# Softmax sums and tap weights in two PSUM tiles, fewer GpSimd taps, wider weight conversions, and an earlier start for four token-mixing tiles

## The chip, the cores and the metric

The kernel runs on one core of one Trainium2 chip. The metric is device time in microseconds (us) of one execution, median of three runs. Engines are named as in the profile: PE (TensorE matmul) and PEld (its weight load), DVE (VectorE), ACT (ScalarE), POOL (GpSimd), SP (SyncE, which here only issues DMAs). A trailing q, as in ACTq, is the engine's queue of DMA issues.

## The reference

Three blocks run one after the other on x of 4 batches, 4224 tokens and 192 features, in fp32.

```
# 1. convolution with weights per token: 8 heads, 7 taps
w = softmax(weight_gen, axis=-1)                    # (4, 4224, 8, 7)
x[b,s,h,:] = sum_k w[b,s,h,k] * x_pad[b, s+k, h, :]
# 2. Fourier mixing and an MLP
mixed = real(fft(fft(x, axis=1), axis=2))
u = x + mixed
x = u + relu(layernorm(u) @ w_ch1) @ w_ch2          # 192 -> 768 -> 192
# 3. token mixing by two 4224 x 4224 matrices
theta = x @ w_theta
y = w_tok_r @ (x*cos(theta)) + w_tok_i @ (x*sin(theta))
u = x + y
out = u + relu(u @ w_ch)
```

The large matrices arrive as fp64 words (passed as int64) and are converted on the chip.

## The kernel before

**Prologue.** Block 1 goes in 32 steps, `g` = 0 to 31: 4 batches of 8 chunks, each chunk 4 or 5 tokens on each of the 128 partitions. Two chunks share one tile `w` of tap weights (`load_w(d)`, d = g // 2). Its softmax is six instructions on DVE and one on ACT: the maximum over the 7 taps (L111), subtract (L113), the exponential on ACT (L114), the sum (L116), add 1e-9 (L118), reciprocal (L120), multiply (L122). The maxima and sums are in `m`, 64 or 72 columns in SBUF. `pool_taps(g)` lets POOL multiply and add the first `NPOOL[c]` of the 7 taps (3 or 4) into `pa` and lets ACT copy the chunk's weights to PSUM (`wps`, L151). `dve_taps(g)` does the rest on DVE: per tap two half-width multiplies (L169), whose weights come from `wps`, and two adds (L178), with two more adds (L174) that take in POOL's `pa`. After the instructions of `dve_taps` whose count is in `SOFT`, one piece of the next softmax is emitted, and after every second one a `step` of the Fourier transforms: `rotated` and `spectrum` on PE, copies on ACT, and joins into `mxt` on DVE (L252, L256). Each engine takes its instructions strictly in the order in which the code emits them.

**Start of the main phase.** `main_phase` walks over steps t, from `T0` = -86. At each t every active generator emits one piece. For t below 0 these are the transforms of the last batch, the conversion of the small weights from fp64 words to a pair of floats, high and low part (`weight`, through `convert`: five ACT and four DVE instructions for each tile, 6 tiles of 256 and 9 of 192 columns), and `prep(k)` for the first token blocks: layer norm, MLP, theta, sine and cosine, and the operand `z`. Block k holds token group k // 2 and batch pair k % 2; `BEGIN` sets its first step, and `load_x(k)` fetches its data. Blocks 0 and 2 hold batches 0 and 1. Blocks 1 and 3 hold batches 2 and 3 and need the last transform, block 3 through DRAM (`mxd`). Tiles `x` have two buffers there.

**Main stream.** From t = 0 PE multiplies `z` by converted tiles of the token matrices (`ws`, 704 columns; `conv(n)` converts tile n, `load_w(n)` fetches its words into `raw`, two buffers) into `y` (L844), one slot of two steps after the other, and DVE adds `y` into `acc` (L431, L433). Slots 0 to 11 use batch pair 0 and the tiles 0 to 3, slots 12 to 23 pair 1 and the same tiles. In this kernel `conv(0)` to `conv(3)` begin at t = -12, -6, 0 and 6 (`2 * u[2] - CONV_STEPS[u[3]]`). This stream runs to the end of the kernel, with `prep` of the later blocks beside it.

Of the kernel before, what the change touches and what calls it, by code (L numbers as in the profile page):

```python
# [10 lines left out]
F32 = mybir.dt.float32  # L11
# [8 lines left out]
PSUM = bass.MemoryType.PSUM  # L20
DRAM = bass.MemoryType.DRAM

B, S, D, H, K, DFF = 4, 4224, 192, 8, 7, 768
P = 128
# [2 lines left out]

SEQ = ((0, 5), (29, 4), (5, 4), (25, 4), (9, 4), (21, 4), (13, 4), (17, 4))
XO = [sum(n + 6 for _, n in SEQ[:c]) for c in range(9)]
SOFT = (0, 1, 4, 6, 8, 10)  # L30
NPOOL = (3, 3, 4, 3, 3, 4, 3, 4)
TCH = 352
NCH = S // TCH
HCH = NCH // 2
PAIR_STEPS = 36
LEAD = 20
BEGIN = {0: -72, 2: -54, 1: -36, 3: -8}
T0, TM, TF = -86, -40, -35
SPARE = (2, 3)
HEAD = 4  # L40
FFT_STEPS = 1
MLP_STEPS = ((13, 14, 17), (15, 16, 19), (18, 19, 22), (21, 22, 25), (24, 25, 28), (27, 28, 31))
NRAW = 2
CONV_STEPS = (18, 12)
BLOCKS = ((0, 0), (1, 0), (0, 1), (1, 1), (2, 1), (1, 2), (2, 2))
OFF = [(31 * j) % 128 if j < NF else (127 - 31 * j) % 128 for j in range(NJ)]
INV2PI = 0.15915494309189535
# [13 lines left out]
def prologue(tc, I, xs, mx, state):  # L61


    nc = tc.nc
    fctx, wctx, actx = ExitStack(), ExitStack(), ExitStack()
# [8 lines left out]
    xp = pool(actx, "px", 3)  # L74
    wp = pool(actx, "pw", 2)
    gp = pool(actx, "pg", 2)
    ps_w = pool(actx, "psw", 2, space=PSUM)
    ps_t = pool(actx, "pst", 3, space=PSUM)

    const = cp.tile([P, NCONST], F32, name="const")  # L80
# [2 lines left out]
    DI = const[:, 844:1100]  # L83
    BD = [const[:119, 1100 + 119 * i : 1219 + 119 * i] for i in range(3)]

    xin, wn, xn, taps = {}, {}, {}, {}
    queue = state["queue"] = collections.deque()

    def load_x(g):
# [7 lines left out]
    def load_w(d):  # L97
        b, c = divmod(d, 4)
        g0, n = 8 * (8 * c + (c > 0)), 8 * (8 + (c == 0))
        w = wp.tile([P, 9 * H, K], F32, tag="w", name=f"w{d}")  # L100
        nc.scalar.dma_start(
            out=w[:, :n].rearrange("p g k -> p (g k)"), in_=I["wg"][b, :, g0 * K : (g0 + n) * K]
        )
        wn[d] = (w, n)

    def softmax(d):
        w, n = wn[d]
        w = w[:, :n]
        m = wp.tile([P, 9 * H], F32, tag="m", name=f"m{d}")[:, :n]
        wide = m.unsqueeze(2).to_broadcast([P, n, K])  # L110
        nc.vector.tensor_reduce(out=m, in_=w, axis=AX.X, op=ALU.max)  # L111
        yield
        nc.vector.tensor_tensor(out=w, in0=w, in1=wide, op=ALU.subtract)  # L113
        nc.scalar.activation(w, w, AF.Exp)  # L114
        yield
        nc.vector.tensor_reduce(out=m, in_=w, axis=AX.X, op=ALU.add)  # L116
        yield
        nc.vector.tensor_scalar(m, m, 1e-9, None, op0=ALU.add)  # L118
        yield
        nc.vector.reciprocal(m, m)  # L120
# [18 lines left out]
    def pool_taps(g):  # L139
        b, c, n, d, jl = place(g)  # L140
        nt = NPOOL[c]
        pa = gp.tile([P, 5, D], F32, tag="pa", name=f"pa{g}")
        for k in range(nt):
            t = pa if k == 0 else gp.tile([P, 5, D], F32, tag="pb", name=f"pb{g}{k}")
            nc.gpsimd.tensor_tensor(  # L145
                out=hv(t, 0, n, None), in0=hv(xin[g], k, n, None), in1=wv(wn[d][0], jl, n, k), op=ALU.mult
            )
            if k:
                nc.gpsimd.tensor_tensor(out=pa[:, :n], in0=pa[:, :n], in1=t[:, :n], op=ALU.add)  # L149
        wps = ps_w.tile([P, 5 * H, K], F32, tag="wps", name=f"wps{g}")  # L150
        nc.scalar.copy(wps[:, : n * H], wn[d][0][:, jl * H : (jl + n) * H])  # L151
        taps[g] = (nt, pa, wps)

    def dve_taps(g):
        b, c, n, d, jl = place(g)
        nt, pa, wps = taps.pop(g)
        if c % 2 == 0:
            xn[d] = np_.tile([P, 9, D], F32, tag="xn", name=f"xn{d}")
        acc = xn[d][:, jl : jl + n]
        halves = [(slice(4 * i, 4 * i + 4), slice(96 * i, 96 * i + 96)) for i in range(2)]  # L160
        ts = [None, None]
        for k in range(nt, K):
            for i, (hs, _) in enumerate(halves):
                if k == nt:
                    o = hv(xn[d], jl, n, hs)
                else:
                    ts[i] = ps_t.tile([P, 5, 96], F32, tag="tmp", name=f"t{g}{k}{i}")
                    o = hv(ts[i], 0, n, None)
                nc.vector.tensor_tensor(out=o, in0=hv(xin[g], k, n, hs), in1=wv(wps, 0, n, k, hs), op=ALU.mult)  # L169
                yield  # L170
            if k == K - 1:
                for i, (_, fs) in enumerate(halves):
                    t = ts[i][:, :n]
                    nc.vector.tensor_tensor(out=t, in0=t, in1=pa[:, :n, fs], op=ALU.add)  # L174
# [134 lines left out]
    load_w(1)  # L309
    run_all(softmax(0))  # L310
    pool_taps(0)
    for g in range(8 * B):
        if g + 2 < 8 * B:
            load_x(g + 2)
        if g % 2 and g // 2 + 2 < 4 * B:
            load_w(g // 2 + 2)
        soft = softmax(g // 2 + 1) if g % 2 == 0 and g // 2 + 1 < 4 * B else iter(())
        if g % 2 and g + 1 < 8 * B:
            pool_taps(g + 1)
        for n, _ in enumerate(dve_taps(g)):  # L320
            if n in SOFT:
                next(soft, None)
            if n % 2:
                step(1)
        if g % 2 == 0 and g + 1 < 8 * B:
            pool_taps(g + 1)
        if g % 2:
            queue.append(rotated(g // 2))
        if g == 16:
            load_words(nc.scalar, wraw, I["wts"])  # L330
        if g % 8 == 7:
            queue.append(spectrum(g // 8))
# [13 lines left out]
def convert(nc, bounds, raw, x, q, t, h, l, loaded=None):  # L346

    words = raw.bitcast(I32).rearrange("p (n t) -> p n t", t=2)[:, :, 0]
    tops = raw.bitcast(U8).rearrange("p (n t) -> p n t", t=8)[:, :, 4]
    x, q = x(), q()
    nc.scalar.copy(x.bitcast(U8), tops)  # L355
    yield
    nc.vector.tensor_scalar(q, x, 0x7F7F7F7F, None, op0=ALU.bitwise_and)  # L357
    yield
    q8 = q.bitcast(U8)
    nc.scalar.activation(q8, q8, AF.Relu, bias=bounds[:, 0:1], scale=-1.0)  # L360
    nc.scalar.activation(q8, q8, AF.Relu, bias=bounds[:, 1:2], scale=-8.0)  # L361
    yield
    nc.vector.scalar_tensor_tensor(q, x, -0x7F7F7F80, q, op0=ALU.bitwise_and, op1=ALU.bitwise_or)  # L363
    yield
    t = t()
    ti = t.bitcast(I32)
    nc.scalar.activation(ti, q.bitcast(I8), AF.Copy, scale=2.0**24)  # L367
# [12 lines left out]
def main_phase(tc, I, xs, mx, out, state):  # L380
    nc = tc.nc
    with ExitStack() as ctx:
# [59 lines left out]

        def buffer(k, tag, shape, name, dt=F32, i=0):
            if k not in SPARE or tag == "r" or (k == 3 and dt is F32 and tag in "xg"):
                return pp.tile([P, *shape], dt, tag=tag, bufs=2 if tag in "xg" else 1, name=name)
            c = places[dt, tag][i]
            t = spare[dt is F32R][:, c : c + int(np.prod(shape))]
            dims = "abcd"[: len(shape)]
            return t.rearrange(f"p ({' '.join(dims)}) -> p {' '.join(dims)}", **dict(zip(dims, shape)))
# [274 lines left out]
        def weight(n, o, h, l):  # L724
            return convert(nc, bounds, wraw[:, o : o + n], *scratch(n, f"w{o}"), lambda: h, lambda: l)
# [5 lines left out]
        start = {}  # L731
        at = lambda t, fn: start.setdefault(t, []).append(fn)
        for n, u in enumerate(units):
            at(2 * u[2] - CONV_STEPS[u[3]], lambda n=n: conv(n))
        for k in order:
            at(begin[k], lambda k=k: prep(k))
        t = T0
        for s in range(2):
            for c in range(3):
                cs = slice(c * 256, (c + 1) * 256)  # L740
                at(t, lambda s=s, c=c, cs=cs: weight(256, s * DFF + c * 256, w1s[:, s, cs], w1s[:, 2 + s, cs]))
                t += 2
        for i in range(9):
            h, l = (w2s[:, i, 0], w2s[:, i, 1]) if i < 6 else (wth[:, 0, i - 6], wth[:, 1, i - 6])
            at(t, lambda i=i, h=h, l=l: weight(D, 2 * DFF + i * D, h, l))
            t += 2

        fin = {}

# [62 lines left out]
        for t in range(T0, 2 * len(slots) + 24):  # L812
            if t <= TM:
                step(FFT_STEPS if t < TM else 1 << 30)
            if t == TM:
                load_x(1)
            if t == BEGIN[3] - 2:
                load_x(3)
            if t == TF:
                state["raw"][0].close()  # L820
# [145 lines left out]
```

## Time and profile before

| | us |
|---|---|
| median of 3 runs (range) | 3408.34 (3407.03 to 3410.01) |
| the profiled execution | 3409.65 |
| span of its trace | 3407.9 |
| busy: PE, DVE, ACT, POOL | 3249.6, 2404.2, 2103.6, 744.3 |
| granted TensorE clock, mean | 0.981 of full speed |

Times in the trace count from the start of the span. What lies around the span in the profiled execution is 1.75 us. PE is busy for 95% of the whole, but this share is a mean over stages that differ: block 1 ends at 343.1 us, the first `y` starts at 437.1 us, and everything after that is the main stream.

### The profile page before, as it was taken

The numbers are of one execution on the slowest core, as the hardware profiler recorded it, in microseconds if no ns is written. First come the engines' busy times: TensorE is split into PE (matmuls) and PEld (weight loads), VectorE is DVE, ScalarE is ACT, GpSimd is POOL, SyncE is SP. The second block draws the span as 40 slices with busy tenths as digits, with TensorE's granted clock in tenths as the row PEclk, the third lists the DMA queues.
The fourth block names the chain that finished last, engine by engine and source line by source line (L and its number), as shares of the span: only waits on it lengthen the run. The fifth ranks groups of instructions, "written<-read, shape, count | busy, mean of one in ns | idle before, by whom it ended". The sixth has DMA issues, their size and how long they took to land.

```text
span 3407.9 us, 54487 instructions
## 1 busy us (share of the span) xinstructions
PE 3249.6 (95%) x20980; PEld 3201.5 (94%) x20980; DVE 2404.2 (71%) x5351; ACT 2103.6 (62%) x3280; POOL 744.3 (22%) x672
## 2 busy tenths in 40 slices
PE   4777779999999999999999999999999999999999
PEld 3667669999999999999999999999999999999999
DVE  8999567667666666666676666666666666666666
ACT  1323656666666666666666666666666666666743
POOL 8999011111111111111111111111111111111123
PEclk8888989999999999999999999999999999999999
DMA  4454123333333333333333333333333333333333
GB/s 158 163 202 152 60 85 109 105 111 112 111 105 111 112 104 111 112 108 107 112 112 106 109 110 105 111 110 103 110 112 112 105 111 112 105 110 112 108 123 121
DMA packets 119668, 388.03 MB, mean 114 GB/s; under 512 B 10096, under 2 KB 64112, under 8 KB 118768
## 3 DMA queue, kind: packets, MB, share of 16 engines
q1 hardware_dynamic: 116672, 376.62, 33.1%
q10 hardware_dynamic: 2736, 7.94, 0.7%
q8 instruction: 164, 2.69, 0.3%
q14 instruction: 96, 0.79, 0.1%
HBM read 351.88 MB, written 32.64 MB: 113 GB/s over the span
## 4 chain that ended last, share of the span: by engine, by line
PE 84%; ACT 1%; DVE 1%; POOL 0%; issue 0%; DMA 0%; POOLq 0%; ACTq 0%; DVEq 0%
PE y L844 66%; PE ch L563 4%; PE fy L787 2%; PE ch L564 2%; PE psh L540 1%; PE psh L539 1%; PE psh L541 1%; PE psh L537 1%; PE psh L538 1%; PE pst L621 1%; PE pst L609 1%; PE psu L513 1%; PE psx L593 0%; ACT cq L360 0%; DVE f L369 0%; ACT cq L361 0%
## 5 line engine op out<-in xcount | busy, mean ns | idle before, releaser
L844 PE MATMUL y<-ws,z 128*128 128x352 f32 x14256 | 2483.3, 325 | 10.0 <-DVE acc L433 6.4
L844 PEld LDWEIGHTS y<-ws,z 128*128 128x128 f32 x14256 | 2275.8, 188 | 13.8 <-DVE acc L433 8.1
L431 DVE TENSOR_TENSOR acc<-y,acc 128x352 f32<-128x352 f32 (+1 forms) x1158 | 597.8, 516 | 121.4 <-PE y L844 121.2
L374 ACT CAST ws<-f 128x704 fp32r<-128x704 f32 x396 | 309.3, 781 | 399.8 <-DVE f L369 394.2
L363 DVE SCALAR_TENSOR_TENSOR cq<-cx,cq 128x176 int32<-128x176 int32 x396 | 135.7, 343 | 472.0 <-ACT cq L361 471.4
L360 ACT ACTIVATE cq<-cq,bounds 128x704 uint8<-128x704 uint8 x396 | 348.6, 880 | 170.9 <-DVE cq L357 164.6
L663 POOL TENSOR_TENSOR r<-r,x 128x256 f32<-128x256 f32 (+1 forms) x260 | 188.4, 757 | 1165.6 <-ACT r L656 1165.6
L367 ACT ACTIVATE f<-cq 128x704 int32<-128x704 int8 x396 | 312.8, 790 | 135.5 <-DVE cq L363 135.4
L376 DVE TENSOR_TENSOR ws<-f,ws 128x704 fp32r<-128x704 f32 x396 | 353.0, 891 | 56.1 <-ACT ws L374 56.0
L369 DVE SCALAR_TENSOR_TENSOR f<-raw,f 128x704 int32<-128x704 int32 x396 | 355.8, 898 | 36.3 <-ACT f L367 36.3
L361 ACT ACTIVATE cq<-cq,bounds 128x704 uint8<-128x704 uint8 x396 | 349.4, 882 | 12.9
L355 ACT COPY cx<-raw 128x704 uint8<-128x704 uint8 x396 | 327.5, 827 | 2.8 <-DMA raw<-in_W 2.8
L550 DVE SCALAR_TENSOR_TENSOR g<-psh,g 128x256 fp32r<-128x256 f32 x384 | 162.2, 422 | 193.1 <-ACT g L549 192.9
L496 POOL TENSOR_SCALAR rs<-mv 128x2 f32<-128x2 f32 x66 | 13.2, 199 | 1188.2 <-DVE mv L495 1158.8
L563 PE MATMUL ch<-w2s,g 128*128 128x384 f32 x768 | 241.1, 350 | 5.5 <-ACT g L549 3.6
L564 PE MATMUL ch<-w2s,g 128*128 128x192 f32 x768 | 194.1, 253 | 0.7 <-DVE g L550 0.5
L674 POOL TENSOR_TENSOR z<-r,z 128x768 fp32r<-128x768 f32 x66 | 122.5, 1856 | 135.2 <-ACT z L669 135.2
L563 PEld LDWEIGHTS ch<-w2s,g 128*128 128x128 f32 x768 | 144.7, 188 | 7.3 <-ACT g L549 5.2
L564 PEld LDWEIGHTS ch<-w2s,g 128*128 128x128 f32 x768 | 146.2, 190 | 2.9 <-DVE g L550 2.7
L149 POOL TENSOR_TENSOR pa<-pa,pb 128x768 f32<-128x768 f32 (+1 forms) x76 | 146.4, 1927 | 6.0
L549 ACT ACTIVATE g<-psh 128x256 fp32r<-128x256 f32 x384 | 142.9, 372 | 2.8 <-PE psh L541 2.8
L145 POOL TENSOR_TENSOR pb<-xin,w 128x768 f32<-128x768 f32 (+1 forms) x76 | 123.2, 1620 | 0.0
(172 smaller groups left out, 3797.6 us busy)
## 6 DMA issues: line engine op xcount, KB each, us to landing
raw<-in_W SPq DMA_DIRECT2D x396, 703.6 KB
xin<-in_xa SPq DMA_DIRECT2D x28, 960.0 KB
out<-fo SPq DMA_DIRECT2D x24, 528.0 KB
mx<-mxd SPq DMA_DIRECT2D x63, 192.0 KB
xs<-xn SPq DMA_DIRECT2D x28, 384.0 KB
mxd<-mxt SPq DMA_DIRECT2D x4, 1632.0 KB
xin<-in_xa SPq DMA_DIRECT2D x4, 1056.0 KB
wraw<-in_wts ACTq DMA_DIRECT2D x1, 3263.6 KB
```

What stands on the lines that cost most here:

```text
L355: nc.scalar.copy(x.bitcast(U8), tops)
L360: nc.scalar.activation(q8, q8, AF.Relu, bias=bounds[:, 0:1], scale=-1.0)
L361: nc.scalar.activation(q8, q8, AF.Relu, bias=bounds[:, 1:2], scale=-8.0)
L367: nc.scalar.activation(ti, q.bitcast(I8), AF.Copy, scale=2.0**24)
L369: nc.vector.scalar_tensor_tensor(ti, words, 5, ti, op0=ALU.logical_shift_right, op1=ALU.bitwise_or)
L374: nc.scalar.copy(h, t)
L376: nc.vector.tensor_tensor(out=l(), in0=t, in1=h.bitcast(F32), op=ALU.subtract)
L431: nc.vector.tensor_tensor(out=d, in0=v, in1=d, op=ALU.add)
L563: nc.tensor.matmul(ch[:, i, 0 : 2 * D], g[:, 0, t], w, start=ft == 0, stop=False)
L564: nc.tensor.matmul(ch[:, i, D : 2 * D], g[:, 1, t], w[:, :D], start=False, stop=ft == 5)
L663: nc.gpsimd.tensor_tensor(out=o[:, ri], in0=o[:, ri], in1=x[:, :, d], op=ALU.mult)
L844: nc.tensor.matmul(ps[:, 0], zz[hl], s[:, hw, ri], start=q + n == 0, stop=q == parts_n - 1 and n == 2)
```

## The change

Six things change; nothing else does.

1. The two PSUM buffers of the tap weights become two named tiles, `wbank0` and `wbank1`, of one bank each. The weights of chunk g lie in `wbank[g % 2]`, and the softmax's `m` lies behind them in `wbank1` (columns 280 on).
2. ACT's copy of the weights is a function of its own, `dve_weights(g)`, and is emitted one step ahead: that of g + 1 ahead of `dve_taps(g)`.
3. `NPOOL` is (3, 3, 3, 3, 3, 3, 3, 4) instead of (3, 3, 4, 3, 3, 4, 3, 4): two chunks of each batch give one tap from POOL to DVE. `SOFT` goes from (0, 1, 4, 6, 8, 10) to (2, 4, 7, 9, 12, 14).
4. `load_w` of the prologue issues on SP instead of ACT.
5. The small weights are converted in 6 tiles (three of 512, three of 576 columns), one each four steps, instead of 15, one each two steps.
6. `conv(0)` to `conv(3)` begin at t = -33, -28, -22 and -16; `load_x(3)` moves from t = -10 to -34, and the `x` tiles get a third buffer.

```diff
-SOFT = (0, 1, 4, 6, 8, 10)
-NPOOL = (3, 3, 4, 3, 3, 4, 3, 4)
+SOFT = (2, 4, 7, 9, 12, 14)
+NPOOL = (3, 3, 3, 3, 3, 3, 3, 4)
-T0, TM, TF = -86, -40, -35
+T0, TM, TF, TX = -86, -40, -35, -34
+EARLY = (-33, -28, -22, -16)
-    ps_w = pool(actx, "psw", 2, space=PSUM)
+    ps_w = pool(actx, "psw", 1, space=PSUM)
+    wbank = [ps_w.tile([P, 512], F32, name=f"wbank{i}") for i in range(2)]
-        nc.scalar.dma_start(
+        nc.sync.dma_start(
             out=w[:, :n].rearrange("p g k -> p (g k)"), ...
-        m = wp.tile([P, 9 * H], F32, tag="m", name=f"m{d}")[:, :n]
+        m = wbank[1][:, 5 * H * K : 5 * H * K + n]
+    def dve_weights(g):
+        wps = wbank[g % 2][:, : 5 * H * K].rearrange("p (q k) -> p q k", k=K)
         nc.scalar.copy(wps[:, : n * H], wn[d][0][:, jl * H : (jl + n) * H])
+        return wps
+        if g + 1 < 8 * B:
+            wpss[g + 1] = dve_weights(g + 1)
         for n, _ in enumerate(dve_taps(g)):
-                return pp.tile(..., bufs=2 if tag in "xg" else 1, name=name)
+                return pp.tile(..., bufs={"x": 3, "g": 2}.get(tag, 1), name=name)
-            at(2 * u[2] - CONV_STEPS[u[3]], lambda n=n: conv(n))
+            at(EARLY[n] if n < HEAD else 2 * u[2] - CONV_STEPS[u[3]], lambda n=n: conv(n))
+        tiles = [(512, [w[:, i * 512 : (i + 1) * 512] for w in w1f]) for i in range(3)]
+        tiles += [(3 * D, [w2s[:, 3 * i : 3 * i + 3, n] for n in range(2)]) for i in range(2)]
+        tiles += [(3 * D, [flat(wth[:, n]) for n in range(2)])]
+        for n, hl in tiles:
+            at(t, lambda n=n, o=o, hl=hl: weight(n, o, *hl))
+            t += 4
-            if t == BEGIN[3] - 2:
+            if t == TX:
                 load_x(3)
```

PE's instructions and their order are the same in both programs. Line numbers of the changed kernel are higher: L111 to L122 become L114 to L125, the copy L151 becomes L158, L169, L174 and L178 become L177, L182 and L186, and a conversion's L355 to L376 become L366 to L389.

DVE in the chunk g = 2, where one tap changes hands and the softmax of `w2` runs; `t250` and `t251` are the two halves of a tap, `pa2` is POOL's part. Before, its first rows:

```order
L169 TENSOR_TENSOR xn1_214<-xin2_128,wps2_187 128x4x96
L111 TENSOR_REDUCE m2_216<-w2_174 128x64
L169 TENSOR_TENSOR xn1_214<-xin2_128,wps2_187 128x4x96
L113 TENSOR_TENSOR w2_174<-w2_174,m2_216 128x448
L169 TENSOR_TENSOR t250_230<-xin2_128,wps2_187 128x384
L169 TENSOR_TENSOR t251_232<-xin2_128,wps2_187 128x384
L178 TENSOR_TENSOR xn1_214<-t250_230,xn1_214 128x4x96
L116 TENSOR_REDUCE m2_216<-w2_174 128x64
```

And in the changed program:

```order
L177 TENSOR_TENSOR xn1_209<-xin2_128,wbank0_97 128x4x96 x2
L177 TENSOR_TENSOR t240_221<-xin2_128,wbank0_97 128x384
L114 TENSOR_REDUCE wbank1_98<-w2_172 128x64
L177 TENSOR_TENSOR t241_224<-xin2_128,wbank0_97 128x384
L186 TENSOR_TENSOR xn1_209<-t240_221,xn1_209 128x4x96
L116 TENSOR_TENSOR w2_172<-w2_172,wbank1_98 128x448
L186 TENSOR_TENSOR xn1_209<-t241_224,xn1_209 128x4x96
L177 TENSOR_TENSOR t250_239<-xin2_128,wbank0_97 128x384
```

DVE now begins with tap 3 (into `xn1`) and not with tap 4, which is in `t240` and `t241`; the maximum stands behind three instructions instead of one, and every `m` is in `wbank1`. L114, which writes it, carries a wait on ACT there that L111 did not.

ACT around the first `z`; `g` are MLP activations, `raw0` and `cx0` belong to `conv(0)`, `r0` is the phase of block 0. Before:

```order
L412 CAST xT0_3215<-psx0_3173 128x384
L549 ACTIVATE spare1_2614<-psh23_3225 128x256
L506 COPY un1_3237<-un1_3237 128x2x64
L549 ACTIVATE spare1_2614<-psh24_3241 128x256
L521 CAST uT1_3268<-psu1_3257 128x512
L549 ACTIVATE spare1_2614<-psh25_3270 128x256
```

And in the changed program, from the same `xT0` on:

```order
L425 CAST xT0_3089<-psx0_3043 128x384
L366 COPY cx0_3105<-raw0_3075 128x704
L562 ACTIVATE spare1_2592<-psh23_3099 128x256
L519 COPY un1_3114<-un1_3114 128x2x64
L371 ACTIVATE cq0_3106<-cq0_3106,bounds_2588 128x704
L372 ACTIVATE cq0_3106<-cq0_3106,bounds_2588 128x704
L562 ACTIVATE spare1_2592<-psh24_3121 128x256
L378 ACTIVATE f0_3143<-cq0_3106 128x704
L534 CAST uT1_3151<-psu1_3138 128x512
L366 COPY cx1_3156<-raw1_3077 128x704
L387 CAST ws0_3167<-f0_3143 128x704
L562 ACTIVATE spare1_2592<-psh25_3159 128x256
```

The conversions of tiles 0 to 3 now stand between the pieces of blocks 0, 2 and 1; before, `cx0` came behind block 0's `z`.

## Rows read from the trace of the kernel before

**Rows 1.** Busy time by stage: stretch, its length, each engine's busy us (instructions), granted clock.

```profile
0.00:343.10 343.10, 230.12 (x1384) 203.25 (x1384) 314.46 (x644) 94.52 (x234) 316.68 (x188) 0.86 0.50 168
343.10:383.80 40.70, 36.63 (x230) 32.51 (x230) 20.55 (x89) 32.88 (x91) 0.90 (x2) 0.92 0.11 32
383.80:419.80 36.00, 28.56 (x172) 23.87 (x172) 22.20 (x66) 17.40 (x46) 5.86 (x9) 0.95 0.29 96
419.80:437.10 17.30, 4.24 (x23) 2.86 (x21) 7.84 (x22) 6.87 (x11) 1.43 (x2) 0.64 0.19 63
437.10:464.10 27.00, 23.67 (x139) 22.03 (x138) 19.87 (x40) 16.32 (x28) 8.86 (x10) 0.92 0.29 93
464.10:505.00 40.90, 33.41 (x189) 29.74 (x190) 26.91 (x61) 23.60 (x34) 5.67 (x7) 0.96 0.22 73
505.00:3200.00 2695.00, 2695.00 (x17646) 2691.37 (x17645) 1857.04 (x4198) 1811.95 (x2715) 345.65 (x427) 1.00 0.33 109
```

**Rows 2.** Groups by line, DVE, 0 to 343.1: count, busy us, mean ns.

```profile
L122 DVE TENSOR_TENSOR w<-w,m 128x448 f32<-128x448 f32 (+1 forms) x16 | 22.6, 1411 | 0.0
L113 DVE TENSOR_TENSOR w<-w,m 128x448 f32<-128x448 f32 (+1 forms) x16 | 21.9, 1372 | 0.0
L118 DVE TENSOR_SCALAR m<-m 128x64 f32<-128x64 f32 (+1 forms) x16 | 10.3, 642 | 0.0
```

**Rows 3.** Timeline of DVE, the first chunks: start us, duration us, instruction.

```profile
8.74 0.20 DVE L118 TENSOR_SCALAR m<-m 128x72 f32<-128x72 f32 x1
9.61 0.68 DVE L122 TENSOR_TENSOR w<-w,m 128x504 f32<-128x504 f32 x1
...
13.54 0.64 DVE L169 TENSOR_TENSOR xn<-xin,wps 128x480 f32<-128x480 f32 x1
14.10 0.62 DVE L113 TENSOR_TENSOR w<-w,m 128x448 f32<-128x448 f32 x1
...
25.65 1.00 DVE L169 TENSOR_TENSOR xn<-xin,wps 128x384 f32<-128x384 f32 x2
26.58 1.01 DVE L169 TENSOR_TENSOR t<-xin,wps 128x384 f32<-128x384 f32 x2
```

**Rows 4.** Waits of DVE, 0 to 343.1: us in total, times, longest us.

```profile
DVE m L111 <- DMA w<-in_wg: 11.8, 3, 5.9
DVE xn L169 <- ACT wps L151: 8.1, 6, 2.1
DVE t L174 <- POOL pa L149: 6.6, 4, 2.4
```

**Rows 5.** Groups by line, POOL, 0 to 343.1.

```profile
L149 POOL TENSOR_TENSOR pa<-pa,pb 128x768 f32<-128x768 f32 (+1 forms) x76 | 146.4, 1927 | 6.0
L145 POOL TENSOR_TENSOR pb<-xin,w 128x768 f32<-128x768 f32 (+1 forms) x76 | 123.2, 1620 | 0.0
```

**Rows 6.** Groups by line, ACT, 343.1 to 392: conversion of the small weights.

```profile
L361 ACT ACTIVATE cqw<-cqw,bounds 128x192 uint8<-128x192 uint8 (+1 forms) x15 | 7.1, 476 | 0.5
...
L367 ACT ACTIVATE fw<-cqw 128x192 int32<-128x192 int8 (+1 forms) x15 | 5.8, 387 | 0.0
```

**Rows 7.** Costliest groups of the page, ACT: the same operations on token tiles.

```profile
L367 ACT ACTIVATE f<-cq 128x704 int32<-128x704 int8 x396 | 312.8, 790 | 135.5 <-DVE cq L363 135.4
...
L361 ACT ACTIVATE cq<-cq,bounds 128x704 uint8<-128x704 uint8 x396 | 349.4, 882 | 12.9
```

**Rows 8.** Timelines of POOL, DVE, ACT and PE around the first products; brackets: idle before, releaser.

```profile
417.92 1.83 POOL L674 TENSOR_TENSOR z<-r,z 128x768 fp32r<-128x768 f32 x1 [0.94 <-ACT z L669]
...
427.67 0.56 DVE L479 TENSOR_TENSOR x<-x,spare 128x384 f32<-128x384 f32 x1 [5.26 <-DMA spare<-mxd]
...
429.07 0.78 ACT L374 CAST ws<-f 128x704 fp32r<-128x704 f32 x1 [6.18 <-DVE f L369]
...
437.10 4.69 PE L844 MATMUL y<-ws,z 128*128 128x352 f32 x15
...
464.10 1.87 PE L844 MATMUL y<-ws,z 128*128 128x352 f32 x10 [1.08 <-POOL z L674]
```

More of the change, by code (lines that the diff above doesn't have):

```diff
@@ L84, in prologue @@
     BD = [const[:119, 1100 + 119 * i : 1219 + 119 * i] for i in range(3)]
-    xin, wn, xn, taps = {}, {}, {}, {}
+    xin, wn, xn, taps, wpss = {}, {}, {}, {}, {}
     queue = state["queue"] = collections.deque()
@@ L149, in pool_taps @@
                 nc.gpsimd.tensor_tensor(out=pa[:, :n], in0=pa[:, :n], in1=t[:, :n], op=ALU.add)
-        wps = ps_w.tile([P, 5 * H, K], F32, tag="wps", name=f"wps{g}")
+        taps[g] = (nt, pa)
+    def dve_weights(g):
+        b, c, n, d, jl = place(g)
+        wps = wbank[g % 2][:, : 5 * H * K].rearrange("p (q k) -> p q k", k=K)
         nc.scalar.copy(wps[:, : n * H], wn[d][0][:, jl * H : (jl + n) * H])
-        taps[g] = (nt, pa, wps)
+        return wps
     def dve_taps(g):
         b, c, n, d, jl = place(g)
-        nt, pa, wps = taps.pop(g)
+        nt, pa = taps.pop(g)
+        wps = wpss.pop(g)
         if c % 2 == 0:
@@ L311, in prologue @@
     pool_taps(0)
+    wpss[0] = dve_weights(0)
     for g in range(8 * B):
@@ L373, in convert @@
     h = h()
+    if len(h.shape) == 3:
+        t = t.rearrange("p (a b) -> p a b", b=h.shape[2])
     nc.scalar.copy(h, t)
@@ L444, in buffer @@
             if k not in SPARE or tag == "r" or (k == 3 and dt is F32 and tag in "xg"):
-                return pp.tile([P, *shape], dt, tag=tag, bufs=2 if tag in "xg" else 1, name=name)
+                return pp.tile([P, *shape], dt, tag=tag, bufs={"x": 3, "g": 2}.get(tag, 1), name=name)
             c = places[dt, tag][i]
@@ L737, in main_phase @@
         t = T0
[L738 to L746, printed above, removed]
+        flat = lambda w: w.rearrange("p s f -> p (s f)")
+        w1f = [flat(w1s[:, 0:2]), flat(w1s[:, 2:4])]
+        tiles = [(512, [w[:, i * 512 : (i + 1) * 512] for w in w1f]) for i in range(3)]
+        tiles += [(3 * D, [w2s[:, 3 * i : 3 * i + 3, n] for n in range(2)]) for i in range(2)]
+        tiles += [(3 * D, [flat(wth[:, n]) for n in range(2)])]
+        o = 0
+        for n, hl in tiles:
+            at(t, lambda n=n, o=o, hl=hl: weight(n, o, *hl))
+            t += 4
+            o += n
         fin = {}
```

## The prediction

> **What bounds the kernel now.** I read the busy time by stage first [rows 1]. From 505 to 3200 us PE is busy without a gap at the full clock, and PE's instructions and their order do not change. So nothing that the change does to other engines can move that part: what counts is when the main stream gets going, and each microsecond saved before 505 us comes off the end. Five stages lie ahead of it, and I take each by its own limit. Block 1, to 343.1 us, has DVE busy for 314.5 and POOL for 316.7 us: both are full. The last transforms, to 383.8, are ACT's (32.9 of 40.7). To 419.8 no engine is full; a chain through the first block ends with its `z`. Then 17.3 us pass in which PE works for 4.2, until the first `y`. From 437.1 to 505 PE has 67.9 us and uses 57.1. Next I read the groups and the waits of DVE and POOL in block 1 [rows 2, 4, 5], since a full engine can be full of waiting for memory, and last the timelines around the first products [rows 8].
>
> **Block 1: the softmax.** Three of DVE's lines stand out [rows 2]: the subtract and the multiply take 1.37 and 1.41 us, the add of 1e-9 0.64. Each has been seen alone [rows 3]: 0.62 us for 448 columns in a gap between two instructions of POOL, 0.68 for 504 and 0.20 for the add before POOL has begun. So the excess is POOL's doing. The products L169, which read one operand from PSUM, do not show it: 0.64 us for 480 columns beside a busy POOL. With `m` in PSUM the three lines are of that kind, and I price them at what they take alone (0.635 as a mean over 448 and 504): 16 x (1.372 - 0.635) = 11.8, 16 x (1.411 - 0.635) = 12.4, 16 x (0.642 - 0.20) = 7.1 us, together 31.3. The bounds are 0 (they stay as they are) and 31.3; I take the upper one, since L169 is the nearest row. Maximum, sum and reciprocal change their place only and stay.
>
> The Trainium skill, Perfetto Trace Analysis, "Optimizing Scalar/DVE Operations", speaks against this: it gives DVE about 60 ns of access time for each instruction on SBUF and about 125 on PSUM. By that the 96 softmax instructions that now touch PSUM would lose an estimated 6 us, and the kernel would take 3377. The trace doesn't show it: the product with a PSUM operand takes 0.64 us for 480 columns, the subtract beside it, all in SBUF, 0.62 for 448 [rows 3], and 32 columns more explain the difference.
>
> **Block 1: the taps.** Two chunks in each of 4 batches give a tap to DVE: 8 taps x 4 half-width instructions = 32. Pairs of them follow each other at 0.93 us [rows 3], so 0.465 each, and DVE gains 14.9 us of work. POOL loses 8 x (1.62 + 1.93) = 28.4 [rows 5]. DVE's work falls by 31.3 - 14.9 = 16.4.
>
> **Block 1: the waits.** DVE waits for 28 us [rows 4]. The 8.1 for ACT's copies come from copies that are emitted at the point of use and stand behind transforms; a step ahead, all but the first 0.5 go. The 6.6 for POOL's `pa` go too, all but 0.3, because POOL then has work for 288 us and DVE for 298. Of the 11.8 for the DMA of `w`, 5.9 are the start; the two others shrink by 0.9 each because the maximum now comes two instructions later. I add 4 us of new waits: transforms follow each other more closely in the same DVE time, and PE, ACT and the exponential can be late. Sum: 16.4 + 7.6 + 6.3 + 1.8 - 4 = 28.1, and block 1 ends at 315.0. POOL, if it kept all its 26.4 us of idle, would end at 343.1 - 28.4 = 314.7, so the two agree. Bounds 18 (14 us of new waits) and 34 (none, and the DMA waits gone). `load_w` on SP stands there behind a load of `xin` and waits for POOL to be done with the older `w`; what is queued behind it is the store of `xn`, which waits for the end of the same chunk on DVE, and so later, anyway. This I price at nothing; it costs about as much as the wait, a few us in all, if POOL falls behind DVE.
>
> **Small weights.** The two groups of a line with different widths give its fixed part: (882 - 476) / (704 - 218) = 0.835 ns a column, so 0.29 us fixed for L361, and likewise 0.21 for L367 [rows 6, 7]; 218 is the mean width over 6 x 256 and 9 x 192. With two instructions of the first kind and three of the second, and 0.08 us of overlap at each start, a tile costs about 0.8 us beside its columns: nine tiles fewer save ACT 7.2. Not all is on the path: before, some tiles trail behind the last transform, whereas now all six fall within it. I take 3, between 0 and 6.
>
> **First products, to 437.1.** Block 3's add waits 5.3 us for a DMA that was issued only after block 0 gave up its buffer, and DVE's part of `conv(0)` stands behind it: ACT idles 6.2 for it, and PE's first `y` comes 17.4 us after block 0's `z` was done [rows 8]. With the third buffer and the load at -34 this wait goes, and the conversions are over before t = 0. Of the 17.3 us of this stage [rows 1] I keep what is block 1's last activations and transpose and block 3's add and layer norm, about 9.5; the wait and 2.5 us of conversion work, 7.8 in all, go. Against that, four tiles of ACT work, each two at 0.88 and three at 0.8 less overlap, 3.8, now stand in the 36 us before, in which ACT is busy for 17.4 [rows 1]. Of these 15 us I let 9 fall into its idle time and 6 lengthen the chain of block 0 and 1 on ACT. Net 2, between -7 (all of it lengthens) and 8 (none does).
>
> **After the first product.** Between 437.1 and 464.1 PE idles 3.3 us and runs part of the time at the low clock [rows 1]; block 1's `z` ends it [rows 8]. There DVE and ACT lose the conversions 1 to 3 (11 us of ACT), and I take 4. The 7.5 us of idle time from 464.1 to 505 belong to conversions from t = 36 on, which stay where they are. Between 0 and 8.
>
> **Sum.** 28 + 3 + 2 + 4 = 37. The profiled execution took 3409.65 (a span of 3407.9 and 1.75 around it), so 3372.6; the median of the runs lies 1.3 below it: 3371.
>
> **Rivals.**
> *The head start is paid back.* The four tiles delay block 0's chain fully (-7) and nothing is won after the first `y`: 28 + 3 - 7 = 24, or 3384. For it: in order, ACT's conversions stand ahead of every activation. Against: ACT is idle for half of that stage.
> *Transforms hold block 1.* PE works 230 us of it at a clock of 0.86 [rows 1], and a shorter block asks for the same in less. If DVE waits 1 us more in each of the 16 pairs of chunks, 21 are left: 3387. Against: PE also waits, and its clock has room to rise.
> *More goes than I allow.* No delay of block 0 and no idle time to 464 and little to 505: 28 + 3 + 8 + 8 = 47, or 3361.
> *Moving `m` does not free it.* `w` is still read and written in SBUF, and if that is what POOL blocks, the 31.3 are not won: 6 are left, 3402, no change that can be told. L169 with `xin` and `xn` in SBUF speaks against it [rows 3].
> *The shared bank makes it slower.* `m` lies in the bank of the odd chunks' weights, and the maximum now waits for ACT's copy of them. That copy is queued behind the transforms' copies. The maximum stands 1.4 us (three instructions) behind the start of its chunk, so a copy that is L late costs 15 x (L - 1.4). The longest lag now is 2.1 us [rows 4], which is 0.7 in a few pairs. From L = 3.9 all 37 us are lost; at 5 it is 54, and the kernel takes 3425. The Trainium skill, PSUM — Partial Sum Buffer, "PSUM bank collisions raise a hardware error", says that two engines must be kept apart by bank and not by address, so by it this wait can't be dropped; no run here shows such a collision.
>
> **How the numbers follow.** Forecast 0.68, head start paid back 0.13, transforms 0.07, more 0.07, not freed 0.03, bank 0.02. What a measurement can tell from no change is 0.2%, 6.8 us: faster 0.95, same 0.03, slower 0.02. The ends of all bounds together would be 3397 and 3352; they will not fall together, and 3358 to 3387 takes in the first three rivals.
>
> **What would show it.** In block 1 the subtract and multiply should take 0.6 us and the add 0.2; waits for `wps` should be gone and the last add should end near 315. The gap from there to the first `y` should go from 94 to about 89 us, with block 0's `z` some us later after the end of block 1 than now (76.7) and no wait of block 3's add for a DMA; from the first `y` to the second half (`z` of block 1) 23 instead of 27. It is wrong if DVE waits for ACT at the maximum, or if L116 and L125 keep 1.4 us.

## The result and the profile after

The changed kernel takes 3373.89 us in the median of 4 runs (3373.53 to 3375.37), the kernel before, beside it, 3407.69 (3406.67 to 3410.01): a ratio of 0.9901, 95% interval 0.9884 to 0.9918. The forecast was 3371 with a range of 3358 to 3387. The profiled execution after took 3375.37 with a span of 3373.6, which is 34.3 us less than the span before. One execution of an experiment below, that with fifteen small tiles, fell into a second, slower state (4839.08 us at a granted clock of 0.61) and is left out of its median.

I read the stages first. The view is the one of [rows 1]: stretch, length, then busy us and instructions of PE, PEld, DVE, ACT and POOL, then the granted clock.

```profile
0.00:315.90 315.90, 219.72 (x1384) 194.86 (x1384) 297.92 (x679) 96.89 (x234) 281.36 (x172) 0.89 0.53 182
315.90:354.20 38.30, 35.31 (x221) 31.41 (x222) 17.89 (x61) 29.89 (x58) 1.35 (x2) 0.92 0.11 33
354.20:397.60 43.40, 31.84 (x180) 27.30 (x178) 26.30 (x68) 26.44 (x49) 6.48 (x9) 0.84 0.41 138
397.60:408.20 10.60, 5.92 (x24) 4.32 (x24) 7.76 (x20) 3.02 (x8) 0.89 (x3) 0.66 0.31 106
408.20:429.84 21.64, 21.47 (x139) 21.18 (x138) 12.00 (x29) 7.50 (x16) 8.22 (x10) 0.94 0.00 1
429.84:470.70 40.86, 33.31 (x188) 29.66 (x189) 27.72 (x63) 23.48 (x34) 5.67 (x8) 0.96 0.22 71
470.70:3165.70 2695.00, 2695.00 (x17646) 2691.38 (x17645) 1856.99 (x4198) 1812.24 (x2714) 345.49 (x427) 1.00 0.33 109
```

The last stretch is the same 2695.00 us as before, gapless in both, and the one ahead of it has kept its length (40.86 for 40.90). All that was won lies before 430 us. The marks of the prediction in us, from both traces (block 1 ends with DVE's last add, which ends at 343.18 before; a `z` is done when POOL's L687 ends; the second half is the first `y` that waits for block 1's `z`):

| | before | after | difference |
|---|---|---|---|
| end of block 1 | 343.2 | 315.9 | -27.3 |
| from there to the store of the last transform | 40.7 | 39.6 | -1.1 |
| from the end of block 1 to block 0's `z` | 76.6 | 81.7 | +5.1 |
| from block 0's `z` to the first `y` | 17.35 | 10.64 | -6.7 |
| from the first `y` to the second half | 27.0 | 21.7 | -5.3 |

In block 1 the three lines of [rows 2] now read as follows (groups by line, DVE, 0 to 320 us; behind the bar busy us and mean ns):

```profile
L125 DVE TENSOR_TENSOR w<-w,wbank 128x448 f32<-128x448 f32 (+1 forms) x16 | 10.3, 646 | 0.0
L116 DVE TENSOR_TENSOR w<-w,wbank 128x448 f32<-128x448 f32 (+1 forms) x16 | 10.3, 642 | 0.0
...
L121 DVE TENSOR_SCALAR wbank<-wbank 128x64 f32<-128x64 f32 (+1 forms) x16 | 3.9, 243 | 0.0
```

54.8 us have become 24.5. Of DVE's waits [rows 4] the first stays, the second is nearly gone, the third is about half of what it was, and one for ACT's `U` has grown, from 1.2 (us in total, times, longest):

```profile
DVE wbank L114 <- DMA w<-in_wg: 9.1, 2, 5.6
...
DVE mxt L260 <- ACT U L286: 3.8, 3, 1.5
DVE t L182 <- POOL pa L152: 3.8, 3, 1.5
...
DVE xn L177 <- ACT wbank L158: 0.5, 1, 0.5
```

POOL, which was nearly full [rows 5], waits longer for DVE: 27.0 us of idle time stand before its first product of a chunk, 22.9 of them for the new weights of L125. Before, they were 18.3 and 13.5 (the first line is of before, the others of after).

```profile
L145 POOL TENSOR_TENSOR pa<-xin,w 128x768 f32<-128x768 f32 (+1 forms) x32 | 51.1, 1596 | 18.3 <-DVE w L122 13.5 <-DMA xin<-in_xa 3.2 <-DVE t L174 1.7
...
L152 POOL TENSOR_TENSOR pa<-pa,pb 128x768 f32<-128x768 f32 (+1 forms) x68 | 126.6, 1862 | 5.3
...
L148 POOL TENSOR_TENSOR pa<-xin,w 128x768 f32<-128x768 f32 (+1 forms) x32 | 50.8, 1586 | 27.0 <-DVE w L125 22.9 <-DMA xin<-in_xa 3.8
```

Around the first products, to be held against [rows 8] (start us, duration us; in brackets idle time before and releaser): block 3's add L492 no longer waits for a DMA, and the second half waits for 0.23 us.

```profile
395.78 1.82 POOL L687 TENSOR_TENSOR z<-r,z 128x768 fp32r<-128x768 f32 x1 [2.03 <-ACT z L682]
...
402.39 0.55 DVE L492 TENSOR_TENSOR x<-x,spare 128x384 f32<-128x384 f32 x1
...
408.24 3.75 PE L858 MATMUL y<-ws,z 128*128 128x352 f32 x15
...
429.90 1.87 PE L858 MATMUL y<-ws,z 128*128 128x352 f32 x10 [0.23 <-POOL z L687]
```

### The profile page after: what moved, and what is told of

It reads as the page before. It is cut to its first block, busy times and chain, and to the rows that moved or that the text cites. A ratio compares the mean times of both kernels' runs of the same rounds, so it can differ in the third digit from the quotient of the medians.

```text
span 3373.6 us, 54383 instructions
## 1 busy us (share of the span) xinstructions
PE 3240.7 (96%) x20980; PEld 3196.1 (95%) x20980; DVE 2379.5 (71%) x5347; ACT 2099.6 (62%) x3235; POOL 709.5 (21%) x656
## 4 chain that ended last, share of the span: by engine, by line
PE 85%; ACT 1%; DVE 1%; POOL 0%; issue 0%; DMA 0%; POOLq 0%; ACTq 0%; DVEq 0%
PE y L858 66%; PE ch L576 4%; PE fy L801 2%; PE ch L577 2%; PE psh L553 1%; PE psh L552 1%; PE psh L554 1%; PE psh L550 1%; PE psh L551 1%; PE pst L634 1%; PE pst L622 1%; PE psu L526 1%; PE psx L606 0%; ACT cq L371 0%; DVE f L380 0%; ACT cq L372 0%
## 5 line engine op out<-in xcount | busy, mean ns | idle before, releaser
L389 DVE TENSOR_TENSOR ws<-f,ws 128x704 fp32r<-128x704 f32 x396 | 353.1, 892 | 57.1 <-ACT ws L387 57.0
L380 DVE SCALAR_TENSOR_TENSOR f<-raw,f 128x704 int32<-128x704 int32 x396 | 354.8, 896 | 33.9 <-ACT f L378 33.8
L366 ACT COPY cx<-raw 128x704 uint8<-128x704 uint8 x396 | 327.1, 826 | 2.2 <-DMA raw<-in_W 2.2
L687 POOL TENSOR_TENSOR z<-r,z 128x768 fp32r<-128x768 f32 x66 | 122.3, 1853 | 134.8 <-ACT z L682 134.8
L562 ACT ACTIVATE g<-psh 128x256 fp32r<-128x256 f32 x384 | 142.7, 372 | 3.4 <-PE psh L554 3.4
L210 PE MATMUL psT<-const,xn 128*128 128x128 f32 x264 | 47.4, 337 | 87.0 <-DVE xn L186 80.4
L210 PEld LDWEIGHTS psT<-const,xn 128*128 128x128 f32 x264 | 41.9, 240 | 91.3 <-issue 57.9
```

## The experiments

All times are medians of 4 executions, of 3 for the fifteen small tiles; no kernel leaves out a part of the reference. The move of `load_w` to SP (item 4) was not undone by itself in any run, and what it is worth stays open. What was open: which edits carry block 1's 27 us, and why block 0's `z` came 5 us later and not 3 while the first `y` gained less than forecast.

### The softmax's sums back in SBUF

```
-        m = wbank[1][:, 5 * H * K : 5 * H * K + n]
+        m = wp.tile([P, 9 * H], F32, tag="m", name=f"m{d}")[:, :n]
```

> The changed kernel with m back in SBUF, all else kept. Theory (the softmax instructions are freed of POOL by having an operand in PSUM): the subtract and the multiply go back to about 1.4 us and the add to 0.64, block 1 ends 25 to 31 us later, at 341 to 347, and the kernel takes 3399 to 3405. Rival (the gain came from the taps, the copies and the waits): the two lines' durations matter little, since DVE then only uses up its slack; block 1 ends at most 5 us later and the kernel takes up to 3379.

3391.63 us, ratio 0.9954 (0.9939 to 0.9968); block 1 ends at 332.7, 16.8 later. DVE's lines:

```profile
L116 DVE TENSOR_TENSOR w<-w,m 128x448 f32<-128x448 f32 (+1 forms) x16 | 20.9, 1305 | 0.0
L125 DVE TENSOR_TENSOR w<-w,m 128x448 f32<-128x448 f32 (+1 forms) x16 | 13.2, 824 | 0.0
...
L121 DVE TENSOR_SCALAR m<-m 128x64 f32<-128x64 f32 (+1 forms) x16 | 7.6, 474 | 0.0
```

```profile
L148 POOL TENSOR_TENSOR pa<-xin,w 128x768 f32<-128x768 f32 (+1 forms) x32 | 51.1, 1597 | 35.6 <-DVE w L125 33.0 <-DMA xin<-in_xa 2.3
```

Between the two expectations. The three lines take 41.7 us for 24.5, and these 17.2 match the 16.8. So PSUM carries 17 us here, not 31: the rest of the 30 by which these lines fell is gained without it. POOL, with fewer taps, idles 35.6 us before its first products in this kernel, 33.0 of them for the weights that L125 is writing, and so the multiply takes 0.82 instead of 1.41: six times, on 448 columns, no instruction of POOL runs beside it, and there it takes 0.61.

### The softmax's old places, with PSUM kept

```
-SOFT = (2, 4, 7, 9, 12, 14)
+SOFT = (0, 1, 4, 6, 8, 10)
```

> The changed kernel with the six softmax instructions back at the places 0, 1, 4, 6, 8 and 10 of a chunk; PSUM tiles, taps and copies as in the changed kernel. Theory (a reader of PSUM is not held up by POOL wherever it stands): subtract and multiply stay at 0.62 to 0.66 us although POOL is busy beside them, POOL gets the next weights earlier and idles less than 33 us, block 1 ends within 4 us of 315.9, and the kernel takes 3370 to 3378. Rival (the places did it: what is short in the changed kernel is short because POOL idles there): the lines go back towards 1.4 us and the kernel takes 3385 to 3400. Rival of the shared bank: the maximum now stands right behind ACT's copy into its bank and waits for it, 1 to 4 us in each of 15 pairs, 3385 to 3430.

3377.05 us, ratio 0.9911 (0.9895 to 0.9928); block 1 ends at 317.7.

```profile
L116 DVE TENSOR_TENSOR w<-w,wbank 128x448 f32<-128x448 f32 (+1 forms) x16 | 10.0, 627 | 0.0
L125 DVE TENSOR_TENSOR w<-w,wbank 128x448 f32<-128x448 f32 (+1 forms) x16 | 10.0, 625 | 0.0
```

```profile
DVE wbank L114 <- DMA w<-in_wg: 12.4, 4, 6.0
```

The theory holds: with the sums in PSUM the lines are short wherever they stand. Both rivals fall; the maximum waits 3.3 us more for its DMA, being earlier, and never for ACT's copy. POOL is busy for 0.5 us or more beside fifteen of the sixteen L116 and ten of the sixteen L125. That POOL would idle less was wrong: 28.7 us before L148, for 27.0.

### The eight taps back to POOL

```
-NPOOL = (3, 3, 3, 3, 3, 3, 3, 4)
+NPOOL = (3, 3, 4, 3, 3, 4, 3, 4)
```

and `SOFT` as before.

> The changed kernel with POOL's eight taps given back to POOL and the softmax's places in a chunk as before. Theory (with the softmax freed, POOL's 317 us of work bind again): DVE waits for POOL's pa, block 1 ends 16 to 28 us later, at 332 to 344, and the kernel takes 3390 to 3402. Rival (DVE sets the end, and its work is 15 us less here): block 1 ends up to 10 us earlier and the kernel takes 3364 to 3374.

3384.81 us, ratio 0.9934 (0.9919 to 0.9949); block 1 ends at 326.5, 10.6 later.

```profile
DVE t L182 <- POOL pa L152: 22.0, 7, 5.8
...
DVE wbank L114 <- ACT wbank L158: 4.4, 2, 3.2
```

The sign is the theory's, by the wait that it named, the size below its 16. But this edit moves the taps and the softmax's places together. The kernel of the part above has the same old places, so the taps alone are what lies between these two: block 1 ends 8.8 later here (326.5 for 317.7). With eight taps fewer DVE has 14.5 us less work (284.6 for 299.1) but waits 19.0 more for `pa`, since POOL binds without them. Here the maximum also waits for ACT's copy in the shared bank, 4.4 us in two chunks: the last rival of the prediction is seen, and small.

### One of the taps back (chunk 5)

```
-NPOOL = (3, 3, 3, 3, 3, 3, 3, 4)
+NPOOL = (3, 3, 3, 3, 3, 4, 3, 4)
```

> The changed kernel with one of the two taps in each of four batches (chunk 5) given back to POOL. Theory (DVE is now the one that sets block 1's end, with POOL idle for 33 us): DVE loses 16 x 0.465 = 7.4 us of work, POOL gains 4 x 3.5 = 14 and stays under DVE; block 1 ends 3 to 7 us earlier and the kernel takes 3367 to 3371. Rival (POOL's idle time is bound to the place of the softmax in each pair of chunks, so a fourth tap makes DVE wait for pa): 3374 to 3381.

3376.79 us, ratio 0.9913 (0.9898 to 0.9928); block 1 ends at 318.2.

```profile
DVE t L182 <- POOL pa L152: 14.1, 6, 4.0
```

The rival is right: the 7.2 us of work taken from DVE (290.8 for 297.9) come back as 10.3 more of waiting for `pa`. POOL's idle time before its first products did take in most of the 13 us of new work, falling from 27.0 to 15.9, but DVE then waits where POOL is late, and the idle time that is left still stands before a new `w`:

```profile
L148 POOL TENSOR_TENSOR pa<-xin,w 128x768 f32<-128x768 f32 (+1 forms) x32 | 50.7, 1586 | 15.9 <-DVE w L125 13.6 <-DMA xin<-in_xa 1.9
```

### The copies at the point of use

```
-        if g + 1 < 8 * B:
-            wpss[g + 1] = dve_weights(g + 1)
...
+        wpss[g] = dve_weights(g)
```

> The changed kernel with ACT's copies of the taps' weights emitted at the chunk that uses them, as before. Theory (emitting a step ahead took away the waits for the copies): DVE waits 5 to 10 us in all for the copies at the first product, block 1 ends 5 to 10 later, and the kernel takes 3379 to 3384. Rival (the two banks alone are enough, since DVE has slack): the waits stay under 2 us and the kernel takes 3373 to 3376.

3376.75 us, ratio 0.9910 (0.9895 to 0.9925); block 1 ends at 317.9, 2.0 later.

```profile
DVE xn L178 <- ACT wbank L159: 9.7, 7, 2.8
...
DVE t L183 <- POOL pa L152: 1.2, 1, 1.2
```

The wait that was to come back did, 9.7 us, but it costs 2: the one for `pa` falls from 3.8 to 1.2, the one for ACT's `U` from 3.8 to nothing, that for the DMA by 0.7. The time lies between the two expectations, close to the rival's 3376, though not by its reason. Here the waits before one engine replaced each other.

### Fifteen small tiles again

The loops over `w1s`, `w2s` and `wth` as before.

> The changed kernel with the small weights in fifteen tiles again. Theory (ACT sets the stage of the last transforms, and wider tiles take fixed parts off it): the last transform comes 1 to 3 us later after the end of block 1 and the kernel takes 3375 to 3377. Rival (the tiles trail behind the transforms and cost nothing): 3373 to 3374.5.

3378.86 us, ratio 0.9919 (0.9902 to 0.9935), 5.0 slower than the change and beyond both expectations. Only its time is read here. The place shows in the traces of before and of the kernel of the next part, which has the wide tiles and the first conversions where they were. ACT's last small tile, before (the last transform's store is at 383.90), and there (at 353.92):

```profile
390.07 0.35 ACT L374 CAST wth<-fw 128x192 fp32r<-128x192 f32 x1 [1.02 <-DVE fw L369]
```

```profile
352.96 0.68 ACT L387 CAST wth<-fw 128x576 fp32r<-128x576 f32 x1
```

Before, the conversion trails 6.5 us behind the last transform, into block 0's chain; with wide tiles it ends just ahead of it.

### The start of the main stream as before, and the early load alone

The first kernel undoes both edits, the second only the conversions:

```
-T0, TM, TF, TX = -86, -40, -35, -34
+T0, TM, TF, TX = -86, -40, -35, -10
...
-bufs={"x": 3, "g": 2}.get(tag, 1)
+bufs=2 if tag in "xg" else 1
...
-            at(EARLY[n] if n < HEAD else 2 * u[2] - CONV_STEPS[u[3]], lambda n=n: conv(n))
+            at(2 * u[2] - CONV_STEPS[u[3]], lambda n=n: conv(n))
```

> The changed kernel with the whole start of the main stream as before: the first four conversions back at -12, -6, 0 and 6, block 3's load back at -10 and two buffers instead of three. Theory (of the two edits to the main stream's start the early load gains and the early conversions lose): the add of block 3 waits some 5 us for its DMA again, the first y comes 5 us later after block 0's z than with the early load alone, and the kernel takes 3374 to 3377, so that all that the two edits bring together is 0 to 3. Rival (the load was hidden anyway, and the conversions alone set the time): 3369 to 3372.

> The changed kernel with the first four conversions back at steps -12, -6, 0 and 6; the third buffer and block 3's load at -34 stay. Theory (moving the conversions costs the chain of block 0 some 5 us and wins 12 around the first product): block 0's z comes 76 to 78 us after the end of block 1 instead of 81.7, the first y 13 to 16 after it instead of 10.6, block 1's z 26 to 27 after that instead of 21.7; the kernel takes 3376 to 3381. Rival (the head start is paid back): 3371 to 3375.

3376.50 us, ratio 0.9911 (0.9894 to 0.9927), and 3369.82 (3368.76 to 3371.81), ratio 0.9892 (0.9875 to 0.9908). All runs of the second are faster than the changed kernel's, which begin at 3373.53, though the intervals of the two ratios overlap. Its timelines:

```profile
384.69 1.84 POOL L687 TENSOR_TENSOR z<-r,z 128x768 fp32r<-128x768 f32 x1 [0.94 <-ACT z L682]
...
389.11 0.55 DVE L492 TENSOR_TENSOR x<-x,spare 128x384 f32<-128x384 f32 x1
...
398.65 3.79 PE L858 MATMUL y<-ws,z 128*128 128x352 f32 x15
...
425.66 1.88 PE L858 MATMUL y<-ws,z 128*128 128x352 f32 x10 [1.11 <-POOL z L687]
```

Counted from the end of block 1 (314.8 in both of these), with the later placings told below:

| the first four conversions at | block 3's load | block 0's `z` | first `y` | second half |
|---|---|---|---|---|
| -12, -6, 0, 6 | -10 | 72.0 | 89.3 | 116.3 |
| -12, -6, 0, 6 | -34 | 71.8 | 83.9 | 110.9 |
| -33, -28, -22, -16 (the change) | -34 | 81.7 | 92.3 | 114.0 |
| -33, -6, 0, 6 | -34 | 75.6 | 85.0 | 112.0 |
| -16, -11, -5, 1 | -34 | 72.4 | 86.4 | 111.3 |

The early load wins 5.2 us between block 0's `z` and the first `y`, which is the DMA wait of [rows 8]; the theory of the first kernel holds. The early conversions cost block 0's chain 9.9, give back 1.5 ahead of the first `y` and 5.3 behind it, and lose 3.1. On the second kernel the theory had the 5.3 right and the rest wrong: block 0's `z` comes earlier than its 76 to 78, the first `y` too. Its rival, that the head start is paid back, has the sign, and more than the head start is paid back: the time is 1.2 us below the rival's range too.

### Other places for the conversions

```
-EARLY = (-33, -28, -22, -16)
+EARLY = (-16, -11, -5, 1)
```

> The changed kernel with the first four conversions at -16, -11, -5 and 1, so that the first begins on ACT just before block 0's z. Theory (a conversion costs block 0's chain only where it stands ahead of that chain's activations, and block 3's add stands behind DVE's part of the first conversion): block 0's z at 72 to 74 us after the end of block 1, the first y 10 to 12 behind it, and the kernel takes 3366 to 3370. Rival (the conversions, wherever they stand, cost ACT what they gain elsewhere): no faster than with the conversions at -12, that is 3370 to 3374.

3372.01 us, ratio 0.9899 (0.9885 to 0.9914). And with `EARLY = (-33, -6, 0, 6)`:

> The changed kernel with only the first conversion early (-33) and the three others at -6, 0 and 6. Theory (each conversion that ACT takes ahead of block 0's z costs that chain some 2.5 us, and only the first one holds up block 3's add): block 0's z at 74 to 75 us after the end of block 1, the first y 10 to 12 us behind it, block 1's z 26 to 27 behind that, and the kernel takes 3368 to 3373. Rival (the chain pays only when ACT is full, and one conversion fits into its gaps): block 0's z at 72, the first y at 82, the kernel takes 3366 to 3368.

3372.51 us (3369.32 to 3373.80), ratio 0.9895 (0.9880 to 0.9910). Of the first the theory held for block 0's `z` only; the first `y` comes 14.0 behind it, not 10 to 12, and the rival has the time. In the second the theory holds, in the time and nearly in its parts: one conversion costs the chain 3.8, more than the 2.5 that it was given, and wins 2.7 between `z` and the first `y`. In the table's last four rows no place of the conversions brings the second half ahead of the 110.9 that it has with all four late. How far a trace can be trusted here shows in the first kernel of the next part, which is the same as the second row's up to the second half: its marks are 72.4, 84.5 and 111.5, so 0.6 us between two traces mean nothing, and the 111.3 of the last row is no loss that can be told.

### The next four conversions earlier, and block 3 earlier

Both start from the kernel with the early load alone.

```
+EARLY = (-12, -6, 0, 6, 27, 34, 41, 48)
```

and `len(EARLY)` for `HEAD` where it is used.

> The changed kernel with the first four conversions at -12, -6, 0 and 6, and the next four at 27, 34, 41 and 48 instead of 36 and the steps after it. Theory (the 7.5 us in which PE idles between block 1's z and the gapless part come from conversions that stand on ACT and DVE between the adds that free the PSUM tiles of y): some of it goes, and the kernel takes 3364 to 3370. Rival (those adds are late because of the next block's chain, or a conversion ahead of its time waits for its ws buffer and blocks ACT): 3370 to 3376.

3374.36 us (3370.39 to 3375.26), ratio 0.9900 (0.9885 to 0.9914). PE's wait for the adds that free the tiles of `y` stays, in more and shorter pieces (6.0 us in 6 pieces without the edit), so the rival is right on the time; its reason was not tested (the kernel without the edit, then the one with it):

```profile
PE y L858 <- DVE acc L446: 6.0, 6, 2.9
```

```profile
PE y L858 <- DVE acc L446: 6.5, 8, 1.5
```

The second edit:

```
-BEGIN = {0: -72, 2: -54, 1: -36, 3: -8}
+BEGIN = {0: -72, 2: -54, 1: -36, 3: -13}
```

> The kernel with the first four conversions at -12, -6, 0 and 6 (block 3's load early), and block 3's preparation begun at -13 instead of -8, so that its add and layer norm stand on DVE ahead of the first conversion's wait for ACT. Theory (with the load early, what holds up the first y is block 3's add and block 1's last add, both behind DVE's wait for a conversion): block 0's z at 72 us after the end of block 1 as before, the first y 8 to 10 us behind it instead of 12.1, and the kernel takes 3364 to 3368. Rival (the first product waits for its converted weights or for the last add of block 1 in any case, and block 3's MLP now stands in ACT's way): the first y still 12 to 13 us behind, 3368 to 3373.

3375.02 us, ratio 0.9904 (0.9888 to 0.9921).

```profile
386.57 1.83 POOL L687 TENSOR_TENSOR z<-r,z 128x768 fp32r<-128x768 f32 x1 [0.94 <-ACT z L682]
...
387.15 1.66 DVE L492 TENSOR_TENSOR x<-x,spare 128x384 f32<-128x384 f32 x1
...
399.50 0.66 PE L606 MATMUL psx<-ident,x 128*128 128x128 f32 x2 [6.02 <-DVE x L592]
...
401.24 1.96 PE L858 MATMUL y<-ws,z 128*128 128x352 f32 x6
```

The theory falls and the rival has the place, though the time is above both. Counted from the end of block 1, block 3's add is 3.1 us earlier, but the first `y` comes 12.8 behind block 0's `z` (12.1 without the edit): PE now waits 6.0 us for block 1's last add L592 (2.3 without the edit), which on DVE stands behind block 3's layer norm and transposed copies and steps of a conversion. The lowest median of all that was run is thus that of the changed kernel without its early conversions.

## Why the prediction was right, and where it was not

**Block 1** was forecast at -28.1 and measured -27.3; kernels with the same block 1 end it between 314.8 and 315.9. Its terms hold, but for the wait for `pa`, of which less than half of the forecast went: the three lines lost 30.3 us (31.3 forecast), DVE's work as a whole fell by 16.5 (16.4), its waits for copies, `pa` and the DMA by 7.6, 2.8 and 2.7 (7.6, 6.3 and 1.8), and the one for ACT's `U` rose by 2.6 (4 of new waits). But these terms are not what each edit is worth. PSUM alone carries 17 us of the 30, the taps, which stand in the sum as a cost, carry 8.8, the places 1.8, and the copies, with 7.6 of waits, 2.0: a wait that goes is not a gain of its size. One row was misread on the way to the right price. The subtract of 0.62 us at 14.10 was not alone: POOL's next instruction starts 0.07 us behind it and takes 2.62 us, where the same shape takes 2.21 at 18.71. So the subtract came first there, and what was longer was POOL's instruction.

```profile
14.17 2.62 POOL L149 TENSOR_TENSOR pa<-pa,pb 128x960 f32<-128x960 f32 x1
...
18.71 2.21 POOL L149 TENSOR_TENSOR pa<-pa,pb 128x960 f32<-128x960 f32 x1
```

**Small weights** were mis-sized: 3 forecast, 4.6 measured at block 0's `z` (76.6 to 72.0 with all else at the main stream's start as before) and 5.0 in the time. The chosen value let less than half of the 7.2 be on the path; in fact the conversion's end moved by 6.8 us against the last transform, from 6.5 behind it to 0.3 ahead, and block 0's `z` gained 4.6.

**First products** is the step that failed. "Of these 15 us I let 9 fall into its idle time and 6 lengthen the chain of block 0 and 1 on ACT": 9.9 lengthened it. The idle time of ACT was counted for the whole stage, but an engine that works in order fills only those gaps in which the conversion's next step is ready, and each step it takes in between delays what stands behind it. And DVE's part of a conversion was not counted at all. Start times of steps of block 0 on its way to `z`, in us from the end of block 1, with the conversions early and late:

| | early (the change) | late | difference |
|---|---|---|---|
| ACT L425, its transposed copy `xT` | 53.72 | 53.00 | 0.72 |
| DVE L642, its phase | 64.75 | 59.95 | 4.80 |
| DVE L663, its clip | 69.31 | 62.79 | 6.52 |
| ACT L668, its angles | 72.41 | 64.18 | 8.23 |
| POOL L687, its `z` | 79.85 | 69.91 | 9.94 |

The first 0.7 are no cost of the conversions, which begin behind it; two kernels with late conversions differ by 0.6 at `z`. So some 9 us are theirs. From the phase to the clip it is DVE that takes in a conversion's steps L380 and L389, 0.89 and 0.88 us. From there on it is ACT. ACT and then DVE of the changed kernel, between block 0's last steps:

```profile
386.64 0.87 ACT L371 ACTIVATE cq<-cq,bounds 128x704 uint8<-128x704 uint8 x1
387.55 0.88 ACT L372 ACTIVATE cq<-cq,bounds 128x704 uint8<-128x704 uint8 x1
388.34 0.51 ACT L668 ACTIVATE r<-r 128x384 f32<-128x384 f32 x1
...
391.09 0.77 ACT L378 ACTIVATE f<-cq 128x704 int32<-128x704 int8 x1
391.77 0.36 ACT L562 ACTIVATE g<-psh 128x256 fp32r<-128x256 f32 x1
...
392.17 0.42 DVE L563 SCALAR_TENSOR_TENSOR g<-psh,g 128x256 fp32r<-128x256 f32 x1 [3.36 <-ACT g L562]
```

Block 0's angles L668 stand behind two steps of a conversion. L562, an activation of block 1's MLP for which DVE waits 3.36 us, stands behind these, the angles and a third step. So the net was not +2 but -3.2 (6.7 won ahead of the first `y`, 9.9 lost), within the bounds of -7 to 8 and nearer to the -7 of the first rival, "the head start is paid back", though that rival is wrong in that nothing would be won after the first `y`. The mark "94 to about 89" came out at 92.3 accordingly.

The granted clock is no rival for these 9.9 us, though it too changed: it is at its lower level (1.2 of 2.4 GHz) from 376.5 to 390.2 in the changed kernel, after PE had waited 1.34 us for DVE, and at the full level until 390.9 in the kernel with the early load alone. Block 0's last matmul ahead of its `z` ends at 374.8, and the steps behind it that are named here wait for ACT, DVE and POOL, not for PE.

**After the first product** 4 were forecast and 5.3 came, 21.7 us for the 23 named.

That the sum, 37, was right to 3 us is luck in part, because the errors have opposite signs: 0.8 too much for block 1, 1.6 too little for the tiles, 5.2 too much for the first products, 1.3 too little behind them.

The 60 and 125 ns of the Trainium skill (Perfetto Trace Analysis, "Optimizing Scalar/DVE Operations") can now be held against pairs. From SBUF (the kernel with the sums back) to PSUM (old places kept in PSUM; the two kernels differ in the places too, but their products take the same 0.56 us) the maximum goes from 622 to 636 ns, the sum from 621 to 630, the reciprocal from 549 to 566. The sign agrees with the page, the size is 9 to 17 ns and not 65; over 48 such instructions 0.6 us.

## What to carry to other kernels

When two engines slow each other, price each edit with the other one done: the PSUM tile and the lighter POOL were each sized against the same stall. Work moved into an in-order engine's idle time costs the chain it stands in unless each of its steps is ready when its gap comes, so count gaps one by one, not the idle time of the stage, and count them on every engine that the work passes. A wait that is taken away is worth only what the next wait on the same engine doesn't take up.

## What the hardware showed that I had not expected

An add on DVE with all operands in SBUF took 1.66 us beside POOL's `z` and 0.55 alone (L492 in the last experiment and in the one with the early load). It began 0.58 us after POOL's 1.83 us instruction and ended 0.41 after that instruction's end. This agrees with the Trainium skill, SBUF — State Buffer, "Who interferes with whom": the one that comes second is held until the first has finished. By the same section an instruction of DVE with only one input in SBUF, outside its two-port modes, isn't held, as the 625 to 627 ns of the softmax lines beside a busy POOL show (old places kept).

DVE's products and their adds (L177, L186) took 577 to 585 ns in the profiled execution of the changed kernel and 554 to 566 in those of six kernels with the same block 1, while pairs still followed each other at about 0.93 us, and DVE was busy for 297.9 us of block 1 there and in the kernel with the early load alone; so a difference of 3% in a mean duration need not show in the time.
